# A short chunk's loads behind four weight rows, and one chunk's transposes moved from the DMA queue to TensorE, in a retention-then-gated-FFN kernel

## The chip, the cores and the metric

One core of one Trainium2 chip runs the whole kernel. The metric is the device time of one execution in microseconds. TensorE is called PE below (PEld: its weight loads), VectorE DVE, ScalarE ACT, GpSimd POOL, SyncE SP; SPq is SP's queue of DMA issues.

## What is computed

Retention (attention with a decaying causal mask instead of a softmax) over 8 batches, 8 heads, 576 tokens and 64 channels a head, and then a feed-forward layer with a sigmoid gate over the 4608 tokens, 512 wide inside and out, 1536 in the middle. All inputs and the output are float32.

```python
scores = scale * np.matmul(q, k.transpose(0, 1, 3, 2))
gamma = 1.0 - 2.0 ** (-5.0 - np.arange(H, dtype=np.float32))
Dmat = np.where(rel >= 0, gamma[:, None, None] ** rel[None, :, :], 0.0)   # rel = query - key
attn = np.matmul(scores * Dmat[None], v)
x = attn.transpose(0, 2, 1, 3).reshape(B * S, H * D)
gate = 1.0 / (1.0 + np.exp(-(x @ w_gate)))
out = (gate * (x @ w_val)) @ w_out
```

## The kernel before

The tokens of a batch are cut into five chunks, four of 128 and a short one of 64, which gives 40 steps, numbered 0 to 39. Steps 0 to 3 are computed in pairs by code of their own. Step 4 is the short chunk of the first batch, step 5 the first chunk of the second batch, and step 6, the seventh, its second. All work is written in the order in which each engine runs it (`manual_schedule`); an engine's queue is that order, and an instruction that waits holds up all behind it on its engine.

For each step from 4 on:

- `load` issues three DMAs from SP for `k`, `q`, `v`. Buffers come from a pool of 18 slots; the list `freed` says whose slot each next load takes, and follows the order of the loads.
- `cast_k`, `cast_q`, `cast_v` on POOL scale by the decay and write bf16 into `qk_nat` (a ring of 4) and `vbd`.
- The transposes of `q` and `k` are made in one of two ways. `cross` is a transposing DMA from SP, `qk_nat` to `T`. `turn` does them on PE: up to eight transposes into one PSUM tile of the pool `qk_psum` (tag `qk`, two buffers), which ACT or DVE then copies to `T`; a full chunk has twelve and so needs two tiles, copied by the two engines given, and the short chunk has eight.
- Phases on PE, in the order of the list `order`: `st0` and `st1` add to the running state (DVE copies it to `sbd`), `qk` makes the scores (DVE masks them into `pt`), `pv` makes the output (ACT copies it to `xT`). `advance` runs the next phase of the list; `qk` of step s also calls `casts_to`, which issues loads, casts and `cross` ahead.

The feed-forward layer runs beside this, in blocks of tokens. `h_units` makes the gate and the value products: for a block of 128 tokens it takes the 12 slices of the middle dimension in pairs, a PSUM tile for each pair, with one sigmoid on ACT and two products `gv` on DVE. It is a generator and gives way after each slice, twice a pair. The output product (`op`) accumulates 12 slices `fc`.

The change lies in the stretch between the two regimes, lines 683 to 760. There the first 512 tokens' `h` products end, chunk 5 is turned on PE, and `op_first` accumulates the `op` products of those 512 tokens in four PSUM banks, four matmuls for each `fc`, with a phase of steps 5 and 4 or a `turn` between them (line 731 holds the matmuls). `cast_wo` turns the rows `ld_o` of the output weights into `wo_sb`, on ACT and DVE by turns. After eight slices, three pairs of `h` of the block at token 512 are put in (`units2`, six steps of the generator), then the last four slices of `op_first`; the four banks are copied to `ob` by ACT and DVE, and the generator goes on. Its first four pairs take their PSUM tiles from `qk_psum`, the last two from the banks that `op_first` used:

```python
units2 = h_units(gvs2, range(NFC), 512, 0, P, [(qk_psum, "qk")] * 4 + [(ffn_psum, "ffn")] * 2)
for i in range(6):
    next(units2)
    ...
op_first(range(8, NFC))
for nb in range(4):
    store(opps[nb], nb * P, 1 + nb, on_dve if nb % 2 else on_act)
for i, _ in enumerate(units2):
    if i in (2, 4):
        advance(at + 1)
```

Lines that the prediction names: 226 `cast_wo`, 254, 264 and 275 the casts of k, q and v, 285 `cast_dense` (a dense copy `vs` of v, on ACT), 291 `cross`, 306 and 308 the transposes and copies of `turn`, 408 `qk`, 427 and 429 `pv`, 431 its copy to `xT`, 441 and 447 the state and its copy, 510 the `h` matmuls, 532 and 540 `gv`, 550 the copies `ob`.

Of the kernel before, what the change touches and what calls it, by code (L numbers as in the profile page):

```python
# [16 lines left out]
def kernel(  # L17
# [19 lines left out]
    nc = tc.nc  # L37

    B, H, S, D = q.shape
# [6 lines left out]
    NFC = DFF // P  # L46
# [29 lines left out]
    freed = [(nm, "pair", A, g) for A in range(2) for nm in "kqv" for g in range(2)]  # L76
    freed += [(nm, 0, i) for nm in "gv" for i in range(2)] + [("g", f, i) for f in (2, 4) for i in range(2)]
    freed += [("v", 2, 0), ("v", 2, 1), ("v", 4, 0), ("g", 6, 0), ("v", 4, 1), ("g", 6, 1), ("v", 6, 0), ("g", 8, 0),
              ("v", 6, 1), ("g", 8, 1), ("g", 10, 0), ("v", 8, 0), ("g", 10, 1), ("v", 8, 1), ("v", 10, 0), ("v", 10, 1)]
    freed += [("k", 5), ("q", 5), ("v", 5), ("o", 0), ("o", 1), ("k", 4), ("q", 4), ("v", 4)]  # L80
    freed += [("o", f) for f in range(2, NFC)]
    for s in range(6, NS):
        freed += [("k", s), ("q", s)] + ([("v", s - 2)] if s > 7 else [])
    slot = {}
# [1 line left out]
    def ld_tile(shape, key):  # L86
        n = len(slot)
        slot[key] = n if n < SLOTS else slot[freed[n - SLOTS]]
        return ld_pool.tile(shape, FP32, tag=f"ld{slot[key]}", name="_".join(["ld"] + [str(x) for x in key]))
# [13 lines left out]
    def load(s):  # L103
        b, c = STEPS[s]
        n = width[c]
        t0 = c * P
        tiles = []
        for nm, src in (("k", k), ("q", q), ("v", v)):
            t = ld_tile([P, H, D], (nm, s))
            nc.sync.dma_start(out=t[0:n], in_=src[b, :, t0:t0 + n, :].rearrange("h p d -> p h d"))  # L110
            tiles.append(t)
        loaded[s] = tiles

# [20 lines left out]
    def load_wo(f):  # L134
        t = ld_tile([P, DM], ("o", f))
        nc.sync.dma_start(out=t, in_=moe_w_out[f * P:(f + 1) * P, :])
        parts["o", f] = t
# [3 lines left out]
    for f in range(0, NFC, 2):  # L141
        load_w(f, 2)
    load(5)
    load(4)
    for f in range(NFC):
        if f == 8:
            load(6)
        load_wo(f)
    LEAD_CAST = 3

# [72 lines left out]
    on_pool, on_act, on_dve = nc.gpsimd.tensor_copy, nc.scalar.copy, nc.vector.tensor_copy  # L223

    def cast_wo(f, eng):
        eng(out=wo_sb[:, f, :], in_=parts.pop(("o", f)))
# [19 lines left out]
    def cast_k(s):  # L246

        b, c = STEPS[s]
        n = width[c]
        k32 = loaded[s][0]  # L250
        kn = qk_nat[s % NB][:, 1:3]
        for j in range(n // 64):
            for hh in range(2):
                nc.gpsimd.tensor_tensor(  # L254
                    out=kn[half(hh), j, :, half(hh)], in0=k32[half(j), hh::2, :],
                    in1=ktab[half(j), c, hh::2].unsqueeze(2).to_broadcast([64, M, D]), op=ALU.mult)
        natural["k", s] = kn

    def cast_q(s):
        b, c = STEPS[s]  # L260
        n = width[c]
        q32 = loaded[s][1]
        qs = qk_nat[s % NB][:, 0].rearrange("p m (hh d) -> p (m hh) d", d=D)
        nc.gpsimd.tensor_tensor(out=qs[0:n], in0=q32[0:n],  # L264
                                in1=qtab[0:n, c, :].unsqueeze(2).to_broadcast([n, H, D]), op=ALU.mult)

    def cast_v(s):

        b, c = STEPS[s]
        n = width[c]  # L270
        v32 = loaded[s][2]
        vb = vbd[s % NB]
        for j in range(n // 64):
            for hh in range(2):
                nc.gpsimd.tensor_copy(out=vb[half(hh), j, :, half(hh)], in_=v32[half(j), hh::2, :])  # L275
        natural["vb", s] = vb

    def cast_dense(s, j):

        if s >= NS or STEPS[s][1] == NC - 1:  # L280
            return
        if j == 0:
            natural["vs", s] = nat_pool.tile([P, 2, M, D], BF16, tag="vs", name=f"vs_{s}", bufs=2)
        for hh in range(2):
            nc.scalar.copy(out=natural["vs", s][half(hh), j], in_=loaded[s][2][half(j), hh::2, :])  # L285

    def cross(s):

        nb = 1 + width[STEPS[s][1]] // 64
        t = att_pool.tile([P, 3, M, P], BF16, tag="T", name=f"T_{s}", bufs=4)  # L290
        nc.sync.dma_start_transpose(out=t[:, 0:nb].rearrange("p j m t -> p (j m) t"),
                                    in_=qk_nat[s % NB][:, 0:nb].rearrange("p j m d -> p (j m d)"))
        turned["q", s] = t[:, 0]
        turned["k", s] = t[:, 1:3]

    def turn(s, engs):

        nb = 1 + width[STEPS[s][1]] // 64
        t = (att_pool.tile([P, 3, M, P], BF16, tag="T", name=f"T_{s}", bufs=4) if nb == 3
             else osb_pool.tile([P, 2, M, P], BF16, tag="osb", name=f"T_{s}"))  # L300
        for b0, eng in zip(range(0, nb, 2), engs):
            n = min(2, nb - b0)
            ps = qk_psum.tile([P, n, M, P], BF16, tag="qk", name=f"Tp_{s}_{b0}")
            for i in range(n):
                for m in range(M):
                    nc.tensor.matmul(ps[:, i, m, :], lhsT=qk_nat[s % NB][:, b0 + i, m, :], rhs=ident,
                                     is_transpose=True, start=(i == 0 and m == 0), stop=(i == n - 1 and m == M - 1))
            eng(out=t[:, b0:b0 + n], in_=ps)
        turned["q", s] = t[:, 0]
        turned["k", s] = t[:, 1:nb]  # L310
# [140 lines left out]
    order = []  # L451
    for s in range(PAIRED, NS):
        if s == PAIRED:

            order += [("st0", 5), ("qk", 5), ("st1", 5), ("qk", 4), ("pv", 5), ("pv", 4)]
        elif s == PAIRED + 1:
            continue
        elif STEPS[s][1] < NC - 1:
            order += [("st0", s), ("qk", s), ("st1", s), ("pv", s)]
        else:  # L460
            order += [("qk", s), ("pv", s)]
# [3 lines left out]
    def loads_to(s):  # L465
        while done["ld"] <= min(NS - 1, s):
            load(done["ld"])
            done["ld"] += 1

    def casts_to(s):  # L470
        while done["cast"] <= min(NS - 1, s):
            x = done["cast"]
            loads_to(x + (1 if x < 16 else 2))
            cast_k(x)
            cast_q(x)
            cross(x)
            cast_v(x)
            done["cast"] += 1

    def run_phase(kind, s):  # L480
        if kind == "qk":
            casts_to(7 if s < 6 else s + LEAD_CAST)
            phase_qk(s)
            if s > 5:
                cast_dense(s + 1, 0)
        elif kind == "pv":
            phase_pv(s)
            if s > 5:
                cast_dense(s + 1, 1)
        else:  # L490
            phase_st(s, int(kind[2]))
# [55 lines left out]
    def store(opp, r0, hold, eng=None):  # L547

        ob = osb_pool.tile([P, DM], FP32, tag="osb", name=f"ob_{r0}")
        (eng or on_act)(out=ob, in_=opp)  # L550
        stores.append([hold if r0 >= LATE else 10 ** 6, r0, ob])
# [40 lines left out]
    def advance(end):  # L592
        nonlocal at
        while at < end:
            run_phase(*order[at])
            at += 1
# [105 lines left out]
    done["cast"] = 6  # L702
    loads_to(7)
    casts_to(6)
    at = 0
    cast_wo(0, on_dve)
# [7 lines left out]
    def op_first(fcs):  # L714
        for fc in fcs:
            if fc == 1:
                advance(at + 1)
                cast_wo(4, on_dve)
            if fc == 2:
                turn(4, [on_act])  # L720
                cast_wo(5, on_act)
                cast_wo(6, on_dve)
                cast_wo(7, on_act)
            if fc in (3, 4, 5, 6):
                advance(at + 1)
            if fc == 7:
                casts_to(8)
            if fc in (9, 11):
                cast_dense(6, (fc - 9) // 2)
            for nb in range(4):  # L730
                nc.tensor.matmul(opps[nb], lhsT=gvs[fc][:, nb * P:(nb + 1) * P], rhs=wo_sb[:, fc, :],  # L731
                                 start=(fc == 0), stop=(fc == NFC - 1))

    op_first(range(8))

    gvs2 = {}
# [6 lines left out]
    cast_wo(10, on_dve)  # L743
    cast_wo(11, on_act)
    op_first(range(8, NFC))
    for nb in range(4):
        store(opps[nb], nb * P, 1 + nb, on_dve if nb % 2 else on_act)
    for i, _ in enumerate(units2):
        if i in (2, 4):
            advance(at + 1)  # L750
    opp = ffn_bank([P, 512], "op_512")
# [53 lines left out]
```

## Time and profile before

| | |
|---|---|
| median of 5 runs | 338.41 us (337.75 to 339.48) |
| the profiled execution | 338.94 us |
| its span, first to last instruction | 337.2 us |
| mean granted clock of TensorE | 0.99 |
| PE busy | 328.6 us, 97% of the span |
| DVE, ACT, POOL busy | 167.7, 172.7, 182.9 us |

A timeline line gives the start in us from the start of the span, the length, engine, line of the code, operation, output and input tiles, shapes and the number of instructions; in brackets stands the idle time of the engine just before, and the engine, tile and line whose end released it. The list of waits gives, after the colon, microseconds in total, how often, and the longest.

### The profile page before, as it was taken

The numbers are of one execution on the slowest core, as the hardware profiler recorded it, in microseconds if no ns is written. First come the engines' busy times: TensorE is split into PE (matmuls) and PEld (weight loads), VectorE is DVE, ScalarE is ACT, GpSimd is POOL, SyncE is SP. The second block draws the span as 40 slices with busy tenths as digits, with TensorE's granted clock in tenths as the row PEclk, the third lists the DMA queues.
The fourth block names the chain that finished last, engine by engine and source line by source line (L and its number), as shares of the span: only waits on it lengthen the run. The fifth ranks groups of instructions, "written<-read, shape, count | busy, mean of one in ns | idle before, by whom it ended". The sixth has DMA issues, their size and how long they took to land.

```text
span 337.2 us, 7584 instructions
## 1 busy us (share of the span) xinstructions
PE 328.6 (97%) x2860; PEld 189.0 (56%) x2860; DVE 167.7 (50%) x353; ACT 172.7 (51%) x355; POOL 182.9 (54%) x327
## 2 busy tenths in 40 slices
PE   7899989999999999999999999999999999999996
PEld 3574456789666556556556655544555455544443
DVE  5838562766456456426446635642664156503320
ACT  7645565657664546365446655445545455323321
POOL 7634847978878785894549966572569400000000
PEclk9959999999999999999999999999999999999999
DMA  7999999999999999999959999982994520020002
GB/s 216 315 348 305 245 255 219 182 193 212 205 199 258 231 248 260 182 272 192 190 147 194 208 245 230 148 178 97 227 205 67 140 66 0 2 93 31 2 31 93
DMA packets 169716, 60.13 MB, mean 178 GB/s; under 512 B 151120, under 2 KB 163664, under 8 KB 169680
## 3 DMA queue, kind: packets, MB, share of 16 engines
q1 hardware_dynamic: 169536, 59.52, 84.3%
q8 instruction: 22, 0.36, 0.4%
q10 hardware_dynamic: 144, 0.13, 0.1%
q14 instruction: 14, 0.11, 0.1%
HBM read 37.75 MB, written 9.44 MB: 140 GB/s over the span
## 4 chain that ended last, share of the span: by engine, by line
PE 91%; SPq 3%; DMA 2%; DVE 1%; ACT 1%; issue 1%; POOL 0%
PE h L510 54%; PE op L578 23%; PE op L731 3%; SPq L119 2%; PE pv L429 2%; PE qk L408 2%; PE pv L427 2%; PE st L441 2%; DMA ld_g<-in_moe_w_gate_dram 2%; PE op L568 1%; PE op L755 1%; ACT vs L285 1%; PE pvp L391 0%; DVE gv L540 0%; ACT g L536 0%
## 5 line engine op out<-in xcount | busy, mean ns | idle before, releaser
L510 PE MATMUL h<-xT,wg_sb 128*128 128x512 bf16 (+3 forms) x584 | 118.8, 326 | 1.0 <-POOL wg_sb L221 0.6
L510 PE MATMUL h<-xT,wv_sb 128*128 128x512 bf16 (+3 forms) x584 | 118.9, 327 | 0.0
L254 POOL TENSOR_TENSOR qk_nat<-ld_k,ktab 64x256 bf16<-64x256 f32 x128 | 78.4, 613 | 55.5 <-PE st L441 28.2
L540 DVE TENSOR_TENSOR gv<-g,h 128x512 bf16<-128x512 bf16 (+1 forms) x106 | 66.3, 626 | 67.2 <-PE h L510 51.3
L536 ACT ACTIVATE g<-h 128x512 bf16<-128x512 f32 (+1 forms) x106 | 58.1, 549 | 73.6 <-PE h L510 67.2
L578 PE MATMUL op<-wo_sb,gv 128*128 128x512 bf16 x360 | 82.8, 379 | 0.0
L510 PEld LDWEIGHTS <-wg_sb 128*128 128x128 bf16 x584 | 52.1, 99 | 38.4 <-POOL wg_sb L221 0.9
L447 DVE CAST sbd<-st 64x256 bf16<-64x256 f32 x112 | 47.1, 420 | 48.9 <-PE st L441 46.4
L510 PEld LDWEIGHTS <-wv_sb 128*128 128x128 bf16 x584 | 51.3, 99 | 33.3
L275 POOL CAST vbd<-ld_v 64x256 bf16<-64x256 f32 x128 | 50.6, 395 | 10.3 <-PE pv L429 5.5
L578 PEld LDWEIGHTS <-gv 128*128 128x128 bf16 x360 | 33.3, 98 | 35.1
L285 ACT CAST vs<-ld_v 64x256 bf16<-64x256 f32 x112 | 45.1, 403 | 1.7
L550 ACT COPY ob<-op 128x512 f32<-128x512 f32 x33 | 19.2, 586 | 43.2 <-PE op L578 37.9
L264 POOL TENSOR_TENSOR qk_nat<-ld_q,qtab 128x512 bf16<-128x512 f32 (+1 forms) x36 | 37.5, 1041 | 2.8
L410 DVE TENSOR_TENSOR pt<-qk,tri 128x512 bf16<-128x512 f32 (+1 forms) x36 | 22.6, 629 | 17.3 <-PE qk L408 16.7
L431 ACT CAST xT<-pv 128x512 bf16<-128x512 f32 (+1 forms) x36 | 19.3, 537 | 20.0 <-PE pv L429 20.0
L441 PEld LDWEIGHTS <-qk_nat 128*128 128x128 bf16 x224 | 14.0, 98 | 9.4
L429 PE MATMUL pv<-pt,vbd 128*128 128x64 bf16 x256 | 19.2, 193 | 0.0
L429 PEld LDWEIGHTS <-vbd 128*128 128x128 bf16 x256 | 16.2, 98 | 3.8
L427 PE MATMUL pv<-T,sbd 128*128 128x64 bf16 x228 | 18.1, 193 | 0.0
L427 PEld LDWEIGHTS <-sbd 128*128 128x128 bf16 x228 | 15.8, 98 | 2.6
L526 ACT ACTIVATE g<-h 128x256 bf16<-128x256 f32 x28 | 10.7, 383 | 11.4 <-PE h L510 9.4
(71 smaller groups left out, 174.8 us busy)
## 6 DMA issues: line engine op xcount, KB each, us to landing
out_dram<-ob SPq DMA_DIRECT2D x35, 256.0 KB, 2.5
ld_k<-in_k_dram SPq DMA_DIRECT2D x28, 256.0 KB, 3.9
ld_q<-in_q_dram SPq DMA_DIRECT2D x28, 256.0 KB, 4.4
ld_v<-in_v_dram SPq DMA_DIRECT2D x28, 256.0 KB, 4.9
ld_g<-in_moe_w_gate_dram SPq DMA_DIRECT2D x12, 256.0 KB, 6.0
ld_v<-in_moe_w_val_dram SPq DMA_DIRECT2D x12, 256.0 KB, 6.3
ld_o<-in_moe_w_out_dram SPq DMA_DIRECT2D x12, 256.0 KB, 5.3
ld_k_pair<-in_k_dram SPq DMA_DIRECT2D x4, 256.0 KB, 4.3
```

The source lines that it names most:

```text
L254: nc.gpsimd.tensor_tensor(out=kn[half(hh), j, :, half(hh)], in0=k32[half(j), hh::2, :], in1=ktab[half(j), c, hh::2].unsqueeze(2).to_broadc ...
L264: nc.gpsimd.tensor_tensor(out=qs[0:n], in0=q32[0:n], in1=qtab[0:n, c, :].unsqueeze(2).to_broadcast([n, H, D]), op=ALU.mult)
L275: nc.gpsimd.tensor_copy(out=vb[half(hh), j, :, half(hh)], in_=v32[half(j), hh::2, :])
L285: nc.scalar.copy(out=natural["vs", s][half(hh), j], in_=loaded[s][2][half(j), hh::2, :])
L410: nc.vector.tensor_tensor(out=pt[:, :, 0:n].rearrange("p m (j t) -> p m j t", t=64), in0=qkp[:, :, 0:n].rearrange("p m (j t) -> p m j t", ...
L427: nc.tensor.matmul(pvp[:, m, half(j)], lhsT=before[:, m, :], rhs=qT[:, m, half(j)], start=True, stop=False)
L429: nc.tensor.matmul(pvp[:, m, half(j)], lhsT=vb[:, j, m, :], rhs=pt[:, m, half(j)], start=before is None, stop=True)
L447: nc.vector.tensor_copy(out=sb[half(hh), :, half(hh)], in_=st_tiles[b][half(hh)])
L510: nc.tensor.matmul(out, lhsT=w_sb[:, kc, fc * P:(fc + 1) * P], rhs=xT[:, kc, t0 + a:t0 + e], start=(kc == 0), stop=(kc == NKC - 1))
L536: nc.scalar.activation(out=g[:, 0:n], in_=h1[:, 0:n], func=AF.Sigmoid)
L540: nc.vector.tensor_tensor(out=gvs[some[0]][:, a:e], in0=g[:, 0:n], in1=h2[:, 0:n], op=ALU.mult)
L578: nc.tensor.matmul(opp, lhsT=gvs[fc][:, nb * P:(nb + 1) * P], rhs=wo_sb[:, fc, :], start=(fc == 0), stop=(fc == NFC - 1))
```

## The change

- The loads of step 4 are issued after the first four rows of the output weights instead of ahead of them, and `freed` is reordered accordingly. `v` of step 5 is loaded by two DMAs of four heads each.
- In the list of phases `pv` of step 5 comes before `qk` of step 4.
- Step 6 is no longer transposed by `cross`; a `turn(6)` with copies on ACT and DVE is put after the first step of the resumed generator.
- In `op_first`, `turn(4)` moves from slice 2 to slice 5, the phases run before slices 3, 4, 6 and 7 instead of 3 to 6, and row 7 of the output weights is cast at slice 5 on DVE instead of at slice 2 on ACT.

```diff
-    freed += [("k", 5), ("q", 5), ("v", 5), ("o", 0), ("o", 1), ("k", 4), ("q", 4), ("v", 4)]
-    freed += [("o", f) for f in range(2, NFC)]
+    freed += [("k", 5), ("q", 5), ("v", 5)] + [("o", f) for f in range(4)] + [("k", 4), ("q", 4), ("v", 4)]
+    freed += [("o", f) for f in range(4, NFC)]
...
-            nc.sync.dma_start(out=t[0:n], in_=src[b, :, t0:t0 + n, :].rearrange("h p d -> p h d"))
+
+            parts_of = 2 if (nm, s) == ("v", 5) else 1
+            for i in range(parts_of):
+                hs = slice(i * H // parts_of, (i + 1) * H // parts_of)
+                nc.sync.dma_start(out=t[0:n, hs], in_=src[b, hs, t0:t0 + n, :].rearrange("h p d -> p h d"))
...
     load(5)
-    load(4)
     for f in range(NFC):
-        if f == 8:
-            load(6)
+        if f in (4, 8):
+            load({4: 4, 8: 6}[f])
         load_wo(f)
...
-            order += [("st0", 5), ("qk", 5), ("st1", 5), ("qk", 4), ("pv", 5), ("pv", 4)]
+            order += [("st0", 5), ("qk", 5), ("st1", 5), ("pv", 5), ("qk", 4), ("pv", 4)]
...
             cast_q(x)
-            cross(x)
+            if x > 6:
+                cross(x)
             cast_v(x)
...
             if fc == 2:
-                turn(4, [on_act])
                 cast_wo(5, on_act)
                 cast_wo(6, on_dve)
-                cast_wo(7, on_act)
-            if fc in (3, 4, 5, 6):
+            if fc == 5:
+                turn(4, [on_act])
+                cast_wo(7, on_dve)
+            if fc in (3, 4, 6, 7):
                 advance(at + 1)
...
     for i, _ in enumerate(units2):
+        if i == 0:
+            turn(6, [on_act, on_dve])
         if i in (2, 4):
             advance(at + 1)
```

## The prediction

> **What bounds the kernel now.** I read the page's shares and chain first, then the list of TensorE's waits, then the timelines of the engines between 40 and 64 us, where every edit lies, and last the clock by stage.
>
> From the page, the busy line and the chain:
>
> ```profile
> PE 328.6 (97%) x2860; PEld 189.0 (56%) x2860; DVE 167.7 (50%) x353; ACT 172.7 (51%) x355; POOL 182.9 (54%) x327
> ...
> PE 91%; SPq 3%; DMA 2%; DVE 1%; ACT 1%; issue 1%; POOL 0%
> ```
>
> TensorE (PE) is the bound: a microsecond added to its queue is a microsecond of the kernel, and only what shortens its work or a wait of its own can save any. The list of PE's waits says how little there is:
>
> ```profile
> PE op L731 <- DVE wo_sb L226: 1.1, 2, 0.9
> ...
> PE h L510 <- DVE gv L540: 0.2, 1, 0.2
> ```
>
> The only waits after the first 20 us that the list has are the two on `wo_sb` (0.86 and 0.21 us) and 0.2 us late in the run. The timeline of PE shows both, and what the chunks' phases cost:
>
> ```profile
> 42.71 0.83 PE L306 MATMUL Tp<-ident,qk_nat 128*128 128x128 bf16 x12
> 43.38 0.28 PE L441 MATMUL st<-vs,qk_nat 128*128 128x64 bf16 x4
> 44.52 1.02 PE L731 MATMUL op<-wo_sb,gv 128*128 128x512 bf16 x4 [0.86 <-DVE wo_sb L226]
> ...
> 46.48 0.61 PE L306 MATMUL Tp<-ident,qk_nat 128*128 128x128 bf16 x8
> 46.93 1.03 PE L731 MATMUL op<-wo_sb,gv 128*128 128x512 bf16 x4
> ...
> 56.26 3.61 PE L731 MATMUL op<-wo_sb,gv 128*128 128x512 bf16 x16 [0.21 <-DVE wo_sb L226]
> ```
>
> Matmuls are pipelined, so a group's time on PE is the step from its start to the next start: 12 transposes 43.38-42.71 = 0.67 us, 8 transposes 0.45, four `op` matmuls 0.86. From 44.52 on the groups follow each other without a hole. The timeline of VectorE (DVE) tells why the 0.86 us wait exists:
>
> ```profile
> 43.12 0.69 DVE L540 TENSOR_TENSOR gv<-g,h 128x512 bf16<-128x512 bf16 x1 [1.17 <-ACT g L536]
> 43.72 0.42 DVE L308 COPY T<-Tp 128x512 bf16<-128x512 bf16 x1
> 44.06 0.42 DVE L226 CAST wo_sb<-ld_o 128x512 bf16<-128x512 f32 x1
> ...
> 59.48 1.29 DVE L550 COPY ob<-op 128x512 f32<-128x512 f32 x2 [2.52 <-PE op L731]
> ```
>
> The first cast of an output weight row starts back to back behind `gv` and the transposes' copy, with no idle time. It waits for its turn on DVE, not for its row: `ld_o` rows are issued from 35.48 us on, and the view of that tile gives for the way from issue to arrival
>
> ```profile
> DMA to landing us min/median/max: 4.6/5.3/6.5
> ```
>
> so row 0 is there by 42.0 us.
>
> **Part by part.**
>
> *Loads.* `load(4)` moves behind four weight rows, `v` of chunk 5 comes as two transfers. By the row above earlier weight rows buy nothing. What comes late is `k` of chunk 4, by four rows: the eight rows take 6.37 us to issue, so about 3.2 us, and its casts on GpSimd (POOL), which now run from 40.14 to 43.3 us, end near 46.5 at the latest. The reader, `turn(4)`, is moved from before `op` group 2 to before group 5, 49.5 us. Cost 0; at its old place, 46.48, `turn(4)` would have met them with no slack. The extra transfer adds one issue, 0.6 us, to SP's queue ahead of the last four rows and chunk 6. POOL already waits for that chunk (4.49 us, until 47.80); at worst its `q`, cast by 51.5, is cast by 52.1, read at 60 us. Cost 0.
>
> *Casts and phases within `op_first`.* Order becomes st0, qk 5, st1, pv 5, then `turn(4)`, qk 4, pv 4. The same matmuls, but `turn(4)` and `qk 4` now have one `op` group between them (0.86 us) where they had two and `st1`. ScalarE (ACT) needs this long:
>
> ```profile
> 47.13 1.01 ACT L308 COPY T<-Tp 128x1024 bf16<-128x1024 bf16 x1 [1.59 <-PE Tp L306]
> 48.04 1.14 ACT L226 CAST wo_sb<-ld_o 128x512 bf16<-128x512 f32 x2
> ```
>
> The copy ends 48.14-46.48 = 1.66 us after the first transpose; handing over to PE takes another 0.04 (cast end 44.48, PE 44.52). PE needs the result 0.45+0.86 = 1.31 us after it. New wait: 1.70-1.31 = **0.39 us**, with everything behind `qk 4` on PE queued behind it. Bounds 0 and 0.8 (ACT with one more cast, 0.6, in front); I take 0.39, since ACT's other copy there, `xT` of pv 5, is over by then. `pv 4` now has one group instead of two before `h` reads its `xT`: ACT finished that 0.80 us after pv 4 began (50.97 to 51.77), the group and pv 4 itself last 1.09, so it is still covered, by some 0.25 us. `cast_wo(7)` goes from ACT to DVE, which is idle from 49.5 to 54.4: 0.
>
> *Chunk 6's transposes.* `cross(6)` leaves SP's queue, where it took 3.17 us of issue before the next loads:
>
> ```profile
> 53.34 3.17 SPq L291 DMA_TRANSPOSE T<-qk_nat  x1
> 56.57 0.56 SPq L110 DMA_DIRECT2D ld_k<-in_k_dram  x1
> ```
>
> Chunk 8's loads can go 3.2 us earlier, but POOL is with chunk 7 until 60.9 us, and PE waited for no `T`. Gain 0. On PE, `turn(6)` is inserted where the pairs of `h` units resume after `op_first`, at 60.16 us of the present timeline, halfway through the fourth pair. Three costs:
>
> 1. 12 transposes, **0.67 us** by the row at 42.71. PE has no hole at 60 us to hide them.
> 2. Room in PSUM. The pool `qk` has two buffers; the third pair and the half-finished fourth hold both. The fourth cannot be given up, since its second half stands behind `turn(6)` in PE's order, so the transposes must take the third's, after DVE's `gv` has read it. Those two `gv` stand behind two `ob` copies on DVE:
>
> ```profile
> 60.68 1.07 DVE L532 TENSOR_TENSOR gv<-g,h 128x128 bf16<-128x128 bf16 x4
> ```
>
> Two of four are done at 60.68+0.54 = 61.22. PE arrives at 60.16: **1.06 us** of waiting. Today PE simply goes on with the fourth pair and nobody waits.
> 3. The second four transposes need a buffer as well, and the only one that comes free is that of the first eight, after ACT's copy: 1.70-0.45 = **1.25 us**, with ACT idle as at 47.13. (The second copy, 0.42 us on DVE, lies under the next `h` groups.)
>
> Bounds: 2 and 3 are 0 if buffers are there after all; 1.6 and 1.9 if DVE or ACT has one more 0.6 us piece in front. I take the rows' values because the order of the code decides them. Sum: 0.67+1.06+1.25+0.39 = **+3.37 us**. The 0.86 and 0.21 us waits stay: no edit touches `gv`, the copy of `T_5` or the casts of rows 0 and 8 on DVE.
>
> *The clock.* PE stands still or transposes for 2.98 us out of 3.4. The windows show a granted clock that fell after a thin stage:
>
> ```profile
> 10.00:20.00 10.00, 8.56 (x190) 5.68 (x187) 6.63 (x12) 6.27 (x13) 5.30 (x8) 0.90 1.13 329
> 20.00:30.00 10.00, 10.00 (x58) 6.04 (x53) 5.86 (x12) 4.51 (x11) 3.68 (x6) 0.76 1.09 348
> 40.00:50.00 10.00, 9.14 (x83) 5.13 (x82) 6.08 (x14) 6.88 (x12) 5.06 (x10) 1.00 0.98 275
> ```
>
> (After the busy columns: clock, DMA share, GB/s.) The loss was 10 x 0.10 + 10 x 0.24 = 3.4 us, after a stage of quarter-array matmuls with many holes; the 0.86 us hole with 20 transposes at 40 to 50 us cost no clock. The new place is dense on both sides, so I take 0 and keep 3.4 as a case of its own. [...]
>
> **The numbers.** The profiled execution took 338.94 us (span 337.2 and 1.7 around it), 0.53 above the median 338.41; a sum of differences holds for both: 342.3 and **341.8**.
>
> **Rivals.**
> - *The waits for room vanish* (buffers come free in time, or the tiles get others): 0.67+0.39 = 1.06, so 339.5. Against it: two buffers, both held. 0.15.
> - *The clock drops a window*: 341.8+3.4 = 345.2. For it the rows at 10 to 30 us, against it the dense neighbourhood. 0.08.
> - *Not slower: output weight rows were the late ones.* If the rows' landing, not DVE's order, ends the 0.86 and 0.21 us waits, the reordered loads remove 1.07 and, if `turn(6)` and `qk 4` also find their data without waiting, the sum is 0.67-1.07 = -0.40, 338.0; with the 0.2 us wait late in the run and the hole of 0.2 us before the third pair (54.72 to 54.98) also gone, under 337.6. It decides only if row 0 lands after 44.06, against the 42.0 worked out above. 0.12: 0.06 same, 0.06 faster by other shifts of this size.
> - *Forecast:* 0.65, its own range 340.7 to 342.8.
>
> The smallest effect a measurement of this kernel can tell is 0.3%, 1.0 us. Faster 0.06; same 0.06 and a little of the first rival's low end, 0.08; slower 0.86. The range takes the forecast and the first rival and leaves out the clock and the not-slower cases: 339.2 to 343.6.
>
> **What would show it.** In the changed profile: two groups of `Tp` (8 and 4) near 61.6 and 63.4 us, the first with about 1.1 us idle before it released by DVE `gv` L532, the second with about 1.2 us released by ACT's copy of `T`; about 0.4 us before `qk` near 51.2 us; the 0.86 us before the first `op` still there; PE's busy time up by 0.7 us. Wrong if the `Tp` groups stand back to back, if the first `op` no longer waits, or if the clock is below 1.00 between 60 and 75 us.

## The result, and the profile after

| | before | after |
|---|---|---|
| median, same chips | 338.71 us (47 runs) | 341.15 us (26 runs) |
| ratio, 95% interval | | 1.0063 (1.0045 to 1.0082) |
| the profiled execution | 338.94 us, clock 0.99 | 339.62 us, clock 1.00 |

The kernel is slower, by 2.1 us by the ratio (0.0063 x 338.71) and by 2.4 us by the medians; the ratio and the table below leave out executions more than 1.5% above the fastest of their kernel. The forecast was 341.8 us.

The list of PE's waits in the profile after (in all, times, longest):

```profile
PE op L736 <- DVE wo_sb L229: 1.7, 3, 0.9
...
PE Tp L309 <- ACT T L311: 1.1, 1, 1.1
PE Tp L309 <- DVE gv L536: 1.0, 1, 1.0
...
PE qk L411 <- ACT T L311: 0.2, 1, 0.2
```

Three releasers are new: the two at `Tp` and the one at `qk`, each where the prediction had put it. The third wait on `wo_sb` is new as well and was not predicted. The timeline of PE:

```profile
40.96 1.02 PE L736 MATMUL op<-wo_sb,gv 128*128 128x512 bf16 x4 [0.86 <-DVE wo_sb L229]
...
45.08 0.19 PE L432 MATMUL pv<-pt,vbd 128*128 128x64 bf16 x1
45.94 1.02 PE L736 MATMUL op<-wo_sb,gv 128*128 128x512 bf16 x4 [0.66 <-DVE wo_sb L229]
...
47.24 1.03 PE L736 MATMUL op<-wo_sb,gv 128*128 128x512 bf16 x4
48.51 0.29 PE L411 MATMUL qk<-T 128*128 128x64 bf16 x4 [0.24 <-ACT T L311]
...
57.55 0.39 PE L514 MATMUL h<-xT,wv_sb 128*128 128x128 bf16 x4
58.92 0.61 PE L309 MATMUL Tp<-ident,qk_nat 128*128 128x128 bf16 x8 [0.99 <-DVE gv L536]
60.63 0.38 PE L309 MATMUL Tp<-ident,qk_nat 128*128 128x128 bf16 x4 [1.10 <-ACT T L311]
60.85 0.39 PE L514 MATMUL h<-xT,wg_sb 128*128 128x128 bf16 x4
```

By the steps from start to start: 48.51-47.24-0.86 = 0.41 us before `qk 4`, 58.92-57.55-0.22 = 1.15 before the first transposes, 60.63-58.92-0.45 = 1.26 before the second, 0.45 + 0.22 = 0.67 for the twelve. That is 3.49 against the predicted 3.37. The new wait before slice 4 of `op` is 45.94-45.08-0.03 = 0.83.

One thing in this timeline is not the change. The first `op` starts at 40.96, 3.56 us earlier than in the profile before, although no work of PE ahead of it was edited. The windows of the profile after give the reason, the clock (after the busy columns: clock, DMA share, GB/s):

```profile
10.00:20.00 10.00, 9.29 (x200) 6.37 (x200) 6.85 (x11) 7.25 (x16) 4.92 (x8) 1.00 1.13 330
20.00:30.00 10.00, 10.00 (x56) 5.31 (x55) 8.64 (x16) 5.19 (x11) 3.92 (x7) 1.00 1.09 348
```

In the profile before these rows had 0.90 and 0.76. Cut into windows of 2 us, its clock reads 0.50 from 18 to 24 us and 0.80 from 24 to 26: one stretch of some 6.8 us at half the clock, called a half-rate stretch below. So the two profiles show executions of two kinds, and their spans, 337.2 and 337.9 us, can't be subtracted. Every execution comes with its mean granted clock, so kernels can be compared at like clock. The table pools the executions of before that were measured beside the experiments; "1.00" is 0.997 and up, "0.99" is 0.985 to 0.992; medians in us, in brackets how many. Some groups are small.

| kernel | clock 1.00 | clock 0.99 |
|---|---|---|
| before | 338.81 (55) | 340.15 (11) |
| after | 339.41 (10) | 343.44 (4) |
| before, unchanged, measured again | 338.82 (5) | 339.17 (2) |
| after without turn(6) | 339.23 (7) | 340.66 (2) |
| before with turn(6) alone | 339.16 (4) | 343.33 (2) |
| after, turn(6) two steps later | 337.32 (8) | 341.27 (2) |
| the same with the old loads | 337.39 (5) | 340.76 (4) |
| the same (new loads) with turn(4) a slice earlier | 336.94 (8) | 340.84 (2) |
| after, turn(6) later, eight fills | 338.73 (11) | none |
| after, turn(6) later, four fills | 338.02 (10) | none |
| before with 3 us of empty matmuls | 339.16 (9) | 342.23 (3) |

At 0.99, the clock that the prediction's profile had, the change costs 343.44-340.15 = 3.3 us; at 1.00 it costs 0.6. The rows also say that a half-rate stretch that takes 3.4 us from PE costs the kernel before only 1.3 us. The experiments had to find out what takes back the rest.

The mixture of clocks differs too. At 0.995 the medians are 339.19 (19) and 341.28 (8). Of all executions 55 of 88 of before stood at 1.00, and 10 of 27 of after. Weighted with before's own shares, the differences at 1.00, 0.995 and 0.99 (0.6, 2.1 and 3.3 us) come to some 1.3 us, an estimate from these rows; the rest of the 2.1 to 2.4 goes with the lower clocks of after's executions. Whether the change brings those or these executions drew them by chance, no run decides.

### The profile page after: what moved, and what is told of

The parts are those of the page before. It is cut to its first block, busy times and chain, and to the rows that moved or that the text cites. A ratio compares the mean times of both kernels' runs of the same rounds, so it can differ in the third digit from the quotient of the medians.

```text
span 337.9 us, 7610 instructions
## 1 busy us (share of the span) xinstructions
PE 327.0 (97%) x2872; PEld 187.9 (56%) x2872; DVE 168.9 (50%) x355; ACT 173.3 (51%) x355; POOL 183.1 (54%) x327
## 4 chain that ended last, share of the span: by engine, by line
PE 85%; DMA 7%; DVE 2%; ACT 2%; POOL 1%; issue 1%; SPq 1%; POOLq 0%
PE h L514 48%; PE op L582 23%; PE pv L432 2%; PE qk L411 2%; DMA ld_o<-in_moe_w_out_dram 2%; PE pv L430 2%; DMA ld_k<-in_k_dram 2%; PE st L444 2%; PE op L736 2%; DMA ld_g<-in_moe_w_gate_dram 2%; DMA ld_k_pair<-in_k_dram 2%; SPq L123 1%; PE op L572 1%; PE op L762 1%; PE pvp L394 1%
## 5 line engine op out<-in xcount | busy, mean ns | idle before, releaser
L514 PE MATMUL h<-xT,wg_sb 128*128 128x512 bf16 (+3 forms) x584 | 117.6, 324 | 0.3 <-DVE gv L544 0.2
L514 PE MATMUL h<-xT,wv_sb 128*128 128x512 bf16 (+3 forms) x584 | 117.5, 324 | 0.0
L411 PEld LDWEIGHTS <-T 128*128 128x128 bf16 x256 | 12.2, 98 | 6.4 <-ACT T L311 0.7
```

Source lines behind the costliest of these rows:

```text
L514: nc.tensor.matmul(out, lhsT=w_sb[:, kc, fc * P:(fc + 1) * P], rhs=xT[:, kc, t0 + a:t0 + e], start=(kc == 0), stop=(kc == NKC - 1))
```

## The experiments

**The kernel before, again** (no edit; the clock of each execution).

> The kernel before, unchanged. It settles how much of the 3.56 us by which the first op matmul starts earlier in the profile after (40.96 against 44.52 us) is the change and how much is the granted clock, which had a half-rate stretch from 18 to 25 us in the profiled execution of before and none in that of after. Clock theory: executions of this same kernel differ in the same way; those at a clock of 1.00 take 336.9 to 337.5 us and those at 0.99 take 338.9 to 340. In one at 1.00 the first op matmuls would wait for the output weight rows, which land at 41.9 us whatever the clock does, so that about 1.3 us of the 3.4 us is not saved. If the change itself removes the half-rate stretch, all executions of this kernel show 0.99.

Median 338.95 us, ratio 0.9995 (0.9976 to 1.0014). Clocks from 0.99 to 1.00 occur here too, so the stretch comes and goes without the change. The 1.00 executions were not at 337 but at 338.8: more than the guessed 1.3 us is lost. The profiled execution had 0.995, and a longer first wait than the 0.9 known:

```profile
PE op L731 <- DVE wo_sb L226: 2.5, 2, 1.9
```

**The changed kernel without turn(6).**

```diff
-            if x > 6:
-                cross(x)
+            cross(x)
...
-        if i == 0:
-            turn(6, [on_act, on_dve])
```

> The changed kernel with chunk 6 transposed by DMA again, as before; loads, phases and casts stay as changed. Theory of the prediction (the room in PSUM and the twelve transposes cost 2.98 us, the wait before qk 4 0.39): 2.4 to 3.0 us under the changed kernel, so about 338.5 to 339. Rival (the order of the loads costs the time: rows 4 to 7 behind chunk 4 land late): within 0.7 us of the changed kernel, about 340.5 to 341.

339.25 us, ratio to before 1.0008 (0.9987 to 1.0029): taking `turn(6)` away gives back nearly all that was lost, some 1.9 us, a little less than expected. At 1.00 it gives back nothing (339.23 against 339.41), and the profile, at 1.00, has a wait that none of the earlier profiles had:

```profile
PE qk L411 <- DMA T<-qk_nat: 1.0, 2, 0.7
```

**The kernel before with turn(6) alone.**

```diff
-            cross(x)
+            if x > 6:
+                cross(x)
...
     for i, _ in enumerate(units2):
+        if i == 0:
+            turn(6, [on_act, on_dve])
```

> The kernel before with one edit alone: chunk 6 transposed on TensorE at the place of the change. Theory of the prediction: 2.6 to 3.0 us over the kernel before (0.67 of transposes, 1.06 and 1.25 of waits for room), 341.3 to 341.7. Rival (the loads): under 1 us over the kernel before.

340.77 us, ratio 1.0048 (1.002 to 1.0075), some 1.6 us where 2.6 to 3.0 were expected: this edit alone makes most of the loss. At 0.99 it costs 343.33-340.15 = 3.2 us, at 1.00 0.35. The two waits for room stand in its profile, at 1.00, at their full size:

```profile
58.40 0.61 PE L306 MATMUL Tp<-ident,qk_nat 128*128 128x128 bf16 x8 [0.99 <-DVE gv L533]
60.11 0.38 PE L306 MATMUL Tp<-ident,qk_nat 128*128 128x128 bf16 x4 [1.10 <-ACT T L308]
```

**The changed kernel with turn(6) two steps later**, when the products of the fourth pair are issued and both PSUM buffers come free.

```diff
     for i, _ in enumerate(units2):
-        if i == 0:
+        if i == 2:
             turn(6, [on_act, on_dve])
```

> The changed kernel with turn(6) two steps of the generator later, when the products of the fourth pair have been issued, so that both PSUM buffers are free or about to be. Theory of the prediction: the two waits, 2.3 us together, shrink to some 0.3 and the kernel is 1.7 to 2.2 us faster than the changed one, about 339.1; the transposes' 0.67 us stay. Rival (loads) or a loss by the transposes themselves: no faster than the changed kernel by more than 0.5 us.

337.54 us, ratio to before 0.9967 (0.9937 to 0.9997), the only version whose interval against before lies wholly under 1. Against the changed kernel it gains 2.1 us at 1.00 and 2.2 at 0.99. The timeline of its PE, at 0.99, shows the twelve transposes in one piece:

```profile
61.85 0.39 PE L514 MATMUL h<-xT,wv_sb 128*128 128x128 bf16 x4
62.33 0.90 PE L309 MATMUL Tp<-ident,qk_nat 128*128 128x128 bf16 x12
63.07 0.28 PE L444 MATMUL st<-vs,qk_nat 128*128 128x64 bf16 x4
```

The wait ahead of them is 62.33-61.85-0.22 = 0.26 us, in place of 1.15 + 1.26. This was the clearest test: two terms of the sum, 2.3 us by prediction, 2.15 by these profiles, 2.1 to 2.2 by time.

**That kernel with the old loads.**

```diff
-    freed += [("k", 5), ("q", 5), ("v", 5)] + [("o", f) for f in range(4)] + [("k", 4), ("q", 4), ("v", 4)]
-    freed += [("o", f) for f in range(4, NFC)]
+    freed += [("k", 5), ("q", 5), ("v", 5), ("o", 0), ("o", 1), ("k", 4), ("q", 4), ("v", 4)]
+    freed += [("o", f) for f in range(2, NFC)]
...
-            parts_of = 2 if (nm, s) == ("v", 5) else 1
+            parts_of = 1
...
+    load(4)
     for f in range(NFC):
-        if f in (4, 8):
-            load({4: 4, 8: 6}[f])
+        if f == 8:
+            load(6)
```

> The kernel with turn(6) two steps later, with the loads of before (chunk 4 ahead of the weight rows, v of chunk 5 in one transfer). Theory now: the load order matters only in executions without a half-rate stretch before 25 us, because there TensorE reaches the first op 3.4 us earlier and ScalarE's dense copies wait for v of chunk 5; in those this kernel is slower than the one with the new loads by 0.3 to 1.1 us (first op waits 1.4 to 2.1 us instead of 1.0, but the 0.8 us wait for row 4 is gone), in those at 0.99 it is equal. Rival, from the prediction: the load order changes nothing in either, within 0.3 us at 1.00 too.

Ratio to before 1.0002 (0.9968 to 1.0036). At 1.00 337.39 against 337.32: equal within the scatter, and my theory of that moment was wrong; the rival, the prediction's own "cost 0", was right. (Its median, 339.26, is higher because only 5 of its 12 executions had 1.00, 8 of 12 in the other.) The theory had counted on the 0.8 us wait for row 4, and that wait stands in the profile after alone: in the four other full-clock profiles with the new loads (without turn(6), turn(4) earlier, eight and four fills) PE does not wait ahead of slice 4.

**That kernel with turn(4) a slice earlier.**

```diff
                 cast_wo(5, on_act)
-                cast_wo(6, on_dve)
-            if fc == 5:
-                turn(4, [on_act])
-                cast_wo(7, on_dve)
             if fc in (3, 4, 6, 7):
                 advance(at + 1)
+            if fc == 4:
+                turn(4, [on_dve])
+                cast_wo(6, on_dve)
+            if fc == 5:
+                cast_wo(7, on_dve)
```

> The kernel with turn(6) two steps later, and turn(4) one slice earlier, behind pv 5, its copy on VectorE, with row 6 cast behind it. Theory: the 0.41 us wait before qk 4 goes in every execution and up to 0.4 us of the wait for row 4 is filled by the transposes: 0.4 to 0.8 us faster than that kernel, about 336.7 at a clock of 1.00. Rival: turn(4) then waits for the late chunk 4 itself (its q is cast by 45.6 us) and nothing is gained, or 0.3 us is lost.

338.14 us, ratio to before 0.9979 (0.9947 to 1.0011). At 1.00 336.94, 0.4 us under its parent, the size of the `qk 4` wait, which its profile no longer has. The gain is not certain by the interval. The profiled execution, at 1.00, took 338.90 us, 2 us over that median, and shows a wait of that size:

```profile
PE qk L411 <- DMA T<-qk_nat: 1.9, 1, 1.9
```

**Fills.** Eight, then four, matmuls of zeros in the first 18 us of the kernel with the later turn(6); they only keep PE busy.

```diff
+    fill(2)
     pair_pv(0, 0, 0)
...
+    fill(2)
     for i in range(2):
         cast_w("g", 0, 2, i, on_pool)
...
+    fill(4)
     h0 = h_units(gvs, (0,), 0, 0, 2 * P)
```

> The kernel with turn(6) two steps later and eight more filling matmuls of zeros between 10 and 17 us, where TensorE has holes. They change no result and only keep TensorE busy. Clock theory: thin work between 11 and 18 us brings the half-rate stretch from 18 to 25 us; with the filling it comes seldom or not at all, so that nearly all executions show a clock of 1.00 and the median is 337.3 to 337.8, with a narrower spread. Rival: the stretch does not depend on the holes; the shares of 1.00, 0.995 and 0.99 stay and the median rises by up to 1 us for the matmuls.

The clock did as expected, 11 of 12 executions at 1.00 and none at 0.99, though against 8 of 12 without the fills that can be chance. The time did not: 338.74 us, since at 1.00 the eight cost 338.73-337.32 = 1.4 of their 1.7 us; by that little of them lay in holes. With the last four alone:

> The kernel with turn(6) two steps later and four filling matmuls of zeros (0.86 us) ahead of the first h unit alone, where TensorE waits 0.3 to 0.9 us for a gate weight cast. Clock theory: these four lie in a hole and lift the busy share of the stage before 18 us, so that executions at 0.99 become rarer than the 2 of 12 of that kernel, at a cost of 0.1 to 0.6 us at 1.00, about 337.6. Rival: the share of 0.99 and 0.995 stays at a third and the fills cost their 0.86 us.

338.14 us, ratio 0.9989 (0.9966 to 1.0012); 10 of 12 at 1.00 against 8 of 12 without fills, too few to tell, and a cost of 0.7 us at 1.00. Inconclusive on the clock, and no gain.

**The kernel before at full clock** (no edit).

> The kernel before once more, for a profile of an execution without the half-rate stretch. Theory: if it has none, the first op waits for its weight row 1.4 to 2.1 us, against 0.86 in the profile that the prediction was made from, qk or another phase waits up to 1.4 us for a T from the DMA queue between 60 and 90 us, as in the kernel without turn(6), and the time is about 338 to 338.7 instead of 335.5. If it has one, no such wait for T.

This execution, at a clock of 0.998 with no early stretch, is the one to set beside the profile after. The time was 339.36, and the wait for the first row only 0.96, but the other expectation came out, larger:

```profile
PE qk L408 <- DMA T<-qk_nat: 2.8, 5, 1.8
...
PE op L731 <- DVE wo_sb L226: 1.1, 2, 1.0
```

The first of the five in the timeline of PE:

```profile
62.97 0.39 PE L510 MATMUL h<-xT,wv_sb 128*128 128x128 bf16 x4
65.16 0.41 PE L408 MATMUL qk<-T 128*128 128x64 bf16 x8 [1.80 <-DMA T<-qk_nat]
```

`qk 7` waits 65.16-62.97-0.22 = 1.97 us for the transposing DMA of chunk 7; by the same steps the next four `qk` lose 0.34, 0.38, 0.42 and 0.56, in all 3.67 us. In the profile of before at 0.99 no `qk` waited:

```profile
66.25 0.39 PE L510 MATMUL h<-xT,wv_sb 128*128 128x128 bf16 x4
66.47 0.40 PE L408 MATMUL qk<-T 128*128 128x64 bf16 x8
```

This is where the clock's 3.4 us go in this execution: PE at full clock runs ahead of a chain of loads, casts and transposing DMAs that hardly moves with TensorE's clock. `qk 6` begins at 58.78 here and at 62.06 in the profile at 0.99, 3.28 us apart, but the transposing DMA of chunk 7 is issued only 0.5 us earlier, here and then at 0.99:

```profile
58.74 2.80 SPq L291 DMA_TRANSPOSE T<-qk_nat  x1
...
59.25 2.71 SPq L291 DMA_TRANSPOSE T<-qk_nat  x1
```

**The kernel before with 3 us of empty work.**

```diff
     for i, _ in enumerate(units2):
+        if i == 0:
+            fill(14)
```

> The kernel before with 14 matmuls of zeros, 14 x 0.216 = 3.0 us of pure TensorE work, at the place where the change puts turn(6); nothing else. Theory: in an execution at full clock TensorE runs ahead of the transposes by DMA and waits 3.7 us for them between 65 and 87 us, so these 3.0 us fall into that wait: within 0.7 us of the kernel before at a clock of 1.00 (338.8), but the full 2.8 to 3.2 us more at 0.99 (340.2 becomes 343.2). Rival: the waits for T went away in the changed kernel because SP's queue is rid of one transpose, and PE work costs its length in every execution: 3 us more at 1.00 as well, 341.8.

Median 339.26 us, ratio 1.0027 (0.9999 to 1.0055): the rival's 3 us, a ratio of 1.009, lies outside. At 1.00 339.16 against 338.81: 3.0 us of PE work cost 0.35. At 0.99 342.23 against 340.15, 2.1 us where 2.8 to 3.2 were expected (three executions; against the three of before measured beside them, 339.39, it is 2.8). The transposes by DMA were all still there, so freeing SP's queue of one is not needed to hide the work at 1.00. That the wait for them is what hides it is read from the other profiles, since the one taken here was at 0.99. Of the full-clock profiles, the three of kernels with `turn(6)` at the place of the change (after, and before with it alone, twice) show no `qk` waiting for the DMA. The kernel before, the one without `turn(6)`, the one with `turn(4)` earlier and the one with four fills show 2.8, 1.0, 1.9 and 2.0 us of it in their lists, the last two although their queue is rid of that transpose as well; the one with eight fills shows none.

**The clock in the kernels with the hole** (no edit: the changed kernel, and before with turn(6) alone). The hole is the 3.1 us around `turn(6)` in which PE waits or transposes.

> The changed kernel once more, for a profile of an execution whose clock is not 1.00. Executions at 0.995 and below 0.985 are commoner in the two kernels with the 3 us hole around turn(6). Theory: the hole itself brings a half-rate stretch of 3.4 or 6.8 us that begins between 61 and 69 us, at a price of 1.7 to 3.4 us. Rival: the only stretch is the early one, 18 to 25 us, as in the kernel before. If this execution runs at 1.00, nothing is settled.

This execution of the changed kernel took 345.79 us at 0.975. Its windows:

```profile
10.00:20.00 10.00, 9.52 (x169) 6.56 (x168) 7.20 (x12) 5.82 (x12) 5.63 (x8) 0.56 1.08 316
20.00:30.00 10.00, 10.00 (x88) 6.79 (x87) 3.86 (x9) 3.44 (x9) 4.37 (x7) 0.59 1.09 348
...
60.00:70.00 10.00, 7.87 (x90) 5.50 (x90) 4.44 (x13) 6.50 (x15) 9.13 (x17) 1.00 0.80 157
```

The half clock lies between 10 and 30 us. The hole around `turn(6)`, now at 63.9 to 67.0, is in the last row, with PE busy 7.87 of 10 us and the clock at 1.00. The rival holds for this execution: the hole, 2.41 us of waiting and 0.67 of transposes, brought no drop here, nor in the next window (1.00 from 70 to 80 us).

> The kernel before with turn(6) alone, once more, for the same question: six of its twelve executions stood at 0.995, one half-rate stretch of 3.4 us. Theory: it begins between 61 and 66 us, right behind the hole. Rival: it begins near 44 us, behind the wait of the first op, as in the execution of the kernel before at 0.995.

This one ran at 1.00 (339.0 us) and settles nothing. Executions at 0.995 stay without a trace in the kernels with the hole; whether the hole ever causes one is open. With 10 of 27 and 4 of 12 executions at 1.00, against 55 of 88 of before, that rival is not refuted.

## Why the prediction was right, and where it was off

The direction and the number held (341.8 forecast, 341.15 measured, range 339.2 to 343.6), but the closeness of the number is in part luck: the waits for `T` at full clock were left out and took most of the loss there, the lower clocks of after's executions were left out and added some, and the two nearly cancelled.

- *The twelve transposes, the two waits for room, the wait before `qk 4`*: 0.67, 1.06, 1.25, 0.39 predicted, 0.67, 1.15, 1.26, 0.41 in the profile after. Moving `turn(6)` removed just the two room waits, and the time fell by them, so these two are shown by experiment; the other two terms stand in the profile at their size.
- *"Gain 0 ... PE waited for no `T`"*: this is the step that failed. It was true of the execution that I had read and false of the full-clock one, where before loses 3.67 us to `T`. PE work added ahead of `qk 7` falls into that wait: 3.0 us of empty work cost 0.35 at a clock of 1.00.
- *"A sum of differences holds for both" the profiled execution and the median*: false for the same reason. The sum is right at the clock of the profile it was made from, 3.3 us against 3.37. At 1.00, from the two full-clock profiles: +0.67 +1.15 +1.26 +0.41, +0.83 for the new wait for row 4, -3.67 for `T`, -0.10 at the first `op` make +0.55. The table has +0.6; the spans of these two, 337.9 and 337.6, differ by 0.3. Each term is that of one execution, and the waits for `T` and for row 4 differ between executions at 1.00, so the agreement is no proof of each.
- *Loads, "cost 0"*: right in the comparison of old and new loads, not in each execution. In the profile after PE, early at full clock, waits 0.83 us for row 4. First that row's cast there, then in before at full clock:

```profile
45.44 0.44 DVE L229 CAST wo_sb<-ld_o 128x512 bf16<-128x512 f32 x1 [2.43 <-DMA ld_o<-in_moe_w_out_dram]
...
44.45 0.43 DVE L226 CAST wo_sb<-ld_o 128x512 bf16<-128x512 f32 x1 [0.68 <-DMA ld_o<-in_moe_w_out_dram]
```

  VectorE stands idle until the row arrives. The row was issued no later than before (38.86 against 39.36 us); it was under way longer, 6.6 us against 5.1, for a reason that no run shows. PE also came to slice 4 sooner, at 45.11 against 45.60: its first `op` began 0.28 us earlier, and `pv 5` now stands ahead of slice 4 where `turn(4)` and `qk 4` stood, 0.21 us less. The prediction had taken rows 4 to 7 as in time because they were in time at 0.99.
- *The 0.86 us before the first `op` stays*: it did, as 0.86. The sign "PE's busy time up by 0.7 us" can't be read from these two profiles (327.0 against 328.6), since matmuls at half the clock count as busy for longer: four 128x256 `h` matmuls from 20.94 us on took 1.06 us in the profile before, at 0.50, and four from 19.17 on 0.60 in the profile after, at 1.00.
- *Rivals.* "The clock drops a window" named a real loss in the wrong place: the half-rate stretches lie between 10 and 30 us in the profile before and in the changed kernel at 0.975, and between 40 and 50 us in before at 0.995, ahead of the new place of `turn(6)`; both kernels have them. What differs is that before hides most of one behind the waits for `T`, and after does not: from 1.00 to 0.99 before rises by 1.3 us, after by 4.0. "The waits for room vanish" and "output weight rows were the late ones" are refuted by the profile after.

## What to carry to other kernels

Before a sum of waits is trusted, ask which kind of execution the profile shows: with another clock an engine meets the transfers at another time, and a wait that one profile lacks can absorb added work in the next (here PE waits 0 us for `T` at 0.99 and 3.67 at full clock, and 3.0 us of empty work cost 0.35 at 1.00). Compare at like clock, and price an inserted step by its room too: with two PSUM buffers and a half-finished pair in one, twelve 56 ns transposes cost 3.1 us at one place and 0.9 two steps later. A queue that never waits in the profile may be only a little ahead, so look how far ahead it is, not only whether it waits.

## What the runs showed of the hardware

TensorE's half-rate stretch varies from execution to execution of one program: none in the profile after, where all windows of 10 us up to 330 us read 1.00, and none in the first 90 us of before at full clock. In others it is reckoned here as time at half the clock, as windows of 2 us show it for the profile before (0.50 from 18 to 24 us). From what windows of 10 us lack it is 6.8 us in the profile before (2 x 10 x (0.10 + 0.24)), some 17 us in the trace at 0.975 (2 x 10 x (0.44 + 0.41)) and 3.4 us in that of before at 0.995 (2 x 10 x 0.17); from span and mean clock alone, 6.8 to 7.5 us in the three of other versions at 0.99 (2 x 339.3 x 0.010, 2 x 340.4 x 0.010, 2 x 338.9 x 0.011). Those of the profile before and of the trace at 0.975 begin in the thin stage or right behind it; the last lies in the stage of the first `op`'s 1.9 us wait, as its window shows:

```profile
40.00:50.00 10.00, 7.85 (x67) 4.60 (x66) 6.10 (x12) 4.94 (x8) 5.78 (x11) 0.83 1.08 307
```

Why this stage lost the clock and the 3.1 us hole of the changed kernel did not (1.00 from 60 to 70 us in both its traces) is open. With eight zero-valued matmuls before 18 us 1 of 12 executions stood below 1.00, without them 4 of 12.
